# A causal tap filter and a gated two-layer product on one core: tap products dealt out between GEMM pairs, and loads, masks and transposes of the ramp rearranged

## The chip, the core and the metric

The kernel runs on one core of one Trainium2 chip. A core has a matrix engine (TensorE, PE in the profile; its weight loads are shown apart as PEld), a vector engine (VectorE, DVE), an engine for activation functions (ScalarE, ACT), a general engine that also issues transfers (GpSimd, POOL) and an engine that only issues transfers (SyncE, SP). They run on their own and wait for one another through semaphores; each takes its instructions in the order of the program. Data lie in HBM outside the core, in SBUF (128 partitions) and in PSUM, where TensorE writes its products. The metric is the device time of one execution in microseconds (us): 698.22, the median of three runs, 698.02 to 698.79.

## What is computed

The input x is 8 sequences of 4,096 tokens of 192 features. Every feature is filtered causally along the sequence with 7 taps; there are 8 sets of taps, one for each group of 24 features, normalised by a softmax. The result, as 32,768 tokens, goes through a layer to 2,048 features, through h * sigmoid(beta * h) with a beta for each of them, and back to 192:

```python
w = np.exp(weight - weight.max(-1, keepdims=True))
w = w / (w.sum(-1, keepdims=True) + 1e-09)              # (8 heads, 7 taps)
x_pad = concatenate([zeros(B, 6, D), x], axis=1)
x_unf = x_pad[:, idx, :].reshape(B, S, 7, 8, 24)        # idx: token + tap
t = einsum('hk,bskhg->bshg', w, x_unf).reshape(B * S, 192)
h = t @ w_in                                            # 192 -> 2048
out = (h / (1 + exp(-beta * h))) @ w_out                # 2048 -> 192
```

## The kernel before

**Tiles and steps.** The tokens are cut into two streams of 16,384 (s = 0, 1), which are worked on together: the 192 features are taken as 64 x 3, and the 64 rows of stream 0 and of stream 1 fill the 128 partitions. The list `steps` cuts each stream into steps of 128, 128 and 256 tokens (steps 0 to 2), then 256 (3 to 8) and then 512 (a tile). In each step the first GEMM gives 16 chunks of 128 hidden features, ScalarE applies Silu with beta as its scale (beta * h * sigmoid(beta * h), hence w_out is divided by beta), and the second GEMM of a step runs inside the next step, spread between that step's first-GEMM pieces by a plan (`mm2_plan`). Its product is copied to SBUF on VectorE (L368) and stored through SP.

**The filter has two forms.** For tile 0, that is steps 0 to 2, which are four blocks of 128 tokens (block 0 for step 0, block 1 for step 1, blocks 2 and 3 for step 2), TensorE does it: `transpose_0` (L202) transposes a block of x in fp32 by three matmuls with an identity, `take_0` (L209) copies it to SBUF as `xr[b]`, `halo_0` (L216) copies its last six tokens to the front of the next block, `conv_0` (L220) multiplies by seven diagonal matrices of the taps, two matmuls for each tap, and `evac_0` (L228) brings the sum to SBUF in bf16 (`xcp`). From tile 1 on VectorE does it: x is loaded in fp32 (`load_x`, L74), cast to bf16 (`cast_x`, L81), transposed by DMA (`transpose_x`, L91, issued on SP), and seven operations per step (L291, L293) multiply and add; the first of these steps is step 3. They are dealt out by `vector_work`, which runs them ahead by a budget in ns.

**Pairs.** In steps 0 to 2 `mm1_pair(i, u)` (L303) works on chunks u and u + 8 at once: six matmuls, three for each half of the partitions, then two activations (L314). The PSUM pool `psum_h` has two buffers, each for one pair. w_in comes in two halves: partitions 0 to 63 get the columns 0 to 1,023 and partitions 64 to 127 the columns 1,024 to 2,047 (`load_w_in`, L109, cast on the way). The other halves, which only steps from 3 on need, are copied within SBUF later (`copy_w_in`, L112).

**The ramp.** Taps, block 0 of x and beta are loaded first. POOL issues the first piece of w_in, builds two masks (`sel`, `ident`: clear, then select), issues the other three pieces, w_out, tile 1 in four loads and the w_in copies, and at last casts the second half of tile 1. SP loads blocks 1 to 3 of x. TensorE runs warm-up matmuls on zeros, the tap product, block 0's transposes, beta's transpose, three warm-ups, block 0's taps, five warm-ups, and then step 0. There, blocks 1 to 3 are transposed after pairs 0, 2 and 6, and the taps of blocks 1 and 2, 14 matmuls each, stand after pairs 1 and 4; those of block 3 stand after the first pair of step 1. `scale_w_out(c)` (L266) divides a chunk of w_out by beta on VectorE: eight chunks in step 0 from pair 4 on, four before and four after block 3's taps in step 1. The second GEMM of step 0 follows in step 1, its first phase after pairs 1 and 2, its second after pairs 5 to 7. The casts and DMA transposes of tile 1's first half stand after pair 4 of step 1, those of the second half after step 1.

Everything is issued through `pin`, so on each engine the order is that of the program's text. On POOL each of the later transfers waits until the transfer eight places before it on that queue has landed.

## Time and profile before

The profiled execution took 697.36 us; the span from its first instruction to its last is 695.6.

| engine | busy us | share of the span | instructions |
|---|---|---|---|
| TensorE matmuls | 686.9 | 99% | 11,559 |
| TensorE weight loads | 538.6 | 77% | 11,559 |
| ScalarE | 587.2 | 84% | 600 |
| VectorE | 541.8 | 78% | 901 |
| GpSimd | 13.7 | 2% | 26 |

A matmul's busy time overlaps that of its neighbours, so its sum says that TensorE is rarely without work, not that it runs at its peak. The granted TensorE clock is 1.000 over the span. The transfers of the ramp, issue and time to landing:

| transfer | queue | number, KB each | first issue | landed after, us |
|---|---|---|---|---|
| x, block 0, two halves | ACT, SP | 2, 96 | 0.73, 1.20 | 2.0 |
| beta | SP | 1, 8 | 1.61 | 3.2 |
| x, blocks 1 to 3 | SP | 3, 192 | 2.07 | 5.3 to 6.0 |
| w_in | POOL | 4, 192 | 1.26, 3.14 | 5.6 to 7.1 |
| w_out | POOL | 4, 384 | 5.02 | 7.7 to 9.1 |
| x, tile 1 | POOL | 4, 192 | 8.03 | 7.6 (median) |
| w_in copies | POOL | 4, 192 | 13.03 | 6.0 to 7.4 |

Over the 3 to 20 us from the span's start the 16 transfer engines are busy nearly all the time; between 5 and 7 us the queue of SP moved 320 packets (768 bytes each) per us, and the queue of POOL, casting w_in in packets of 1 KB, 62 to 132 per us from 6 to 9 us and 214 in the next.

### The profile page before, as it was taken

Reading aid. Unit: us, or ns where it says so; the run is one execution under the profiler, and the core shown is the slowest. Engines: PE = TensorE matmul, PEld = TensorE weight load, DVE = VectorE, ACT = ScalarE, POOL = GpSimd, SP = SyncE. Lnnn points to the kernel's source line nnn. Section 1 sums busy time; section 2 is a strip of 40 time slices with the busy share of each in tenths; the row PEclk is TensorE's granted clock in tenths of the full one; section 3 lists DMA queues with packets and bytes.
Section 4 is the critical chain, followed back from the end, with each engine's and each line's share of the span. In section 5 each row is a group of like instructions: output and inputs, shape, how many; then the busy total and the mean of one; then the engine's idle time right before and its main releaser. Section 6 shows DMA issues by size and latency. Waiting matters only on the chain.

```text
span 695.6 us, 25420 instructions
## 1 busy us (share of the span) xinstructions
PE 686.9 (99%) x11559; PEld 538.6 (77%) x11559; DVE 541.8 (78%) x901; ACT 587.2 (84%) x600; POOL 13.7 (2%) x26
## 2 busy tenths in 40 slices
PE   8999999999999999999999999999999999999998
PEld 6699996777777777777777777777777777777777
DVE  4799999999988788778798778797788797785002
ACT  5899999888888888888888888888888888888881
POOL 7000000000000000000000000000000000000000
PEclk9999999999999999999999999999999999999999
DMA  9654433443423334233334233334323342211112
GB/s 228 142 132 115 116 102 100 106 125 104 131 70 104 99 104 115 75 89 98 98 105 115 72 90 100 98 104 116 78 79 104 98 105 70 60 36 47 36 37 69
DMA packets 121196, 67.33 MB, mean 97 GB/s; under 512 B 55024, under 2 KB 120384, under 8 KB 121088
## 3 DMA queue, kind: packets, MB, share of 16 engines
q1 hardware_dynamic: 119152, 61.67, 32.8%
q0 software_dynamic: 1792, 3.93, 2.4%
q8 instruction: 90, 1.47, 0.9%
q14 instruction: 18, 0.15, 0.1%
q10 hardware_dynamic: 144, 0.10, 0.1%
HBM read 28.32 MB, written 25.17 MB: 77 GB/s over the span
## 4 chain that ended last, share of the span: by engine, by line
PE 92%; DVE 5%; DMA 1%; issue 1%; SPq 0%; POOL 0%; DVEq 0%; POOLq 0%
PE po L360 45%; PE ph L323 45%; DVE acc L293 3%; PE po L383 2%; DMA w_in_s<-in_moe_w_in_dram 1%; DVE w_out_s L267 1%; DVE xb L84 1%; PE po L224 0%; DVE acc L291 0%; DMA xt<-xb 0%; SPq L95 0%; DVE o_sb L368 0%; PE ph L310 0%; DVE xcp L235 0%; PE po L206 0%
## 5 line engine op out<-in xcount | busy, mean ns | idle before, releaser
L326 ACT ACTIVATE g<-ph,beta 128x1024 bf16<-128x1024 f32 (+1 forms) x544 | 560.8, 1039 | 85.0 <-PE ph L323 81.2
L360 PEld LDWEIGHTS <-g 64*128 64x128 bf16 x7936 | 361.1, 94 | 94.6 <-issue 1.3
L360 PE MATMUL po<-w_out_s,g 64*128 64x192 bf16 x7936 | 427.1, 243 | 0.7 <-DVE o_sb L368 0.5
L323 PE MATMUL ph<-xc,w_in_s 64*128 64x512 bf16 (+1 forms) x3264 | 419.0, 357 | 0.7 <-DVE xc L293 0.7
L293 DVE SCALAR_TENSOR_TENSOR acc<-xt,tapn,acc 128x512 f32<-128x512 bf16 (+1 forms) x450 | 315.4, 764 | 0.9
L323 PEld LDWEIGHTS <-w_in_s 64*128 64x128 bf16 x3264 | 167.7, 94 | 47.5 <-PE po L360 0.9
L368 DVE COPY o_sb<-po 128x384 f32<-128x384 f32 x124 | 69.1, 557 | 129.0 <-PE po L360 127.1
L293 DVE SCALAR_TENSOR_TENSOR xc<-xt,tapn,acc 128x512 bf16<-128x512 bf16 (+1 forms) x90 | 64.2, 765 | 0.2
L84 DVE CAST xb<-xf 128x768 bf16<-128x768 f32 (+1 forms) x62 | 49.0, 831 | 0.0
L291 DVE TENSOR_SCALAR acc<-xt,tapn 128x512 f32<-128x512 bf16 (+1 forms) x90 | 40.5, 501 | 3.0 <-DMA xt<-xb 1.9
L314 ACT ACTIVATE g<-ph,beta 128x256 bf16<-128x256 f32 (+1 forms) x48 | 22.0, 562 | 5.6 <-PE ph L310 5.2
L310 PE MATMUL ph<-xcp,w_in_s 64*128 64x256 bf16 (+1 forms) x144 | 14.5, 306 | 2.1 <-ACT g L314 1.5
L310 PEld LDWEIGHTS <-w_in_s 64*128 64x128 bf16 x144 | 6.9, 94 | 5.9 <-issue 3.4
L383 PE MATMUL po<-w_out_s,g 128*128 128x192 bf16 x128 | 10.7, 246 | 0.0
L383 PEld LDWEIGHTS <-g 128*128 128x128 bf16 x128 | 10.5, 98 | 0.2 <-issue 0.2
L386 DVE COPY o_sb<-po 128x192 f32<-128x192 f32 x8 | 2.9, 358 | 7.6 <-PE po L383 7.6
L235 DVE TENSOR_SCALAR xcp<-po,rsum 128x384 bf16<-128x384 f32 x7 | 4.0, 611 | 4.5 <-PE po L224 4.5
L224 PE MATMUL po<-xr,diag 64*128 64x384 f32 x49 | 7.1, 379 | 0.3 <-DVE xr L214 0.2
L224 PEld LDWEIGHTS po<-xr,diag 64*128 64x128 f32 x49 | 5.7, 204 | 1.1 <-DVE xr L214 1.1
L282 DVE COPY xt<-xt 128x18 bf16<-128x18 bf16 x28 | 4.7, 166 | 0.0
L267 DVE TENSOR_SCALAR w_out_s<-w_out_f,rbeta 128x192 bf16<-128x192 f32 x16 | 4.5, 353 | 0.0
L178 PE MATMUL ph<-zeros 128*128 128x256 bf16 (+1 forms) x16 | 3.1, 363 | 1.1 <-DVE xr L167 1.1
(44 smaller groups left out, 36.9 us busy)
## 6 DMA issues: line engine op xcount, KB each, us to landing
out_dram<-o_sb SPq DMA_DIRECT2D x124, 192.0 KB, 2.7
xf<-in_x_dram SPq DMA_DIRECT2D x60, 384.0 KB, 4.3
xt<-xb SPq DMA_TRANSPOSE x124, 2.4
w_out_f<-in_moe_w_out_dram POOLq DMA_DIRECT2D x4, 384.0 KB, 8.4
w_in_s<-in_moe_w_in_dram POOLq DMA_DIRECT2D x4, 192.0 KB, 6.6
xf<-in_x_dram POOLq DMA_DIRECT2D x4, 192.0 KB, 7.7
w_in_s<-w_in_s POOLq DMA_DIRECT2D x4, 192.0 KB, 7.0
out_dram<-o_sb SPq DMA_DIRECT2D x8, 96.0 KB, 1.6
```

The source lines that it names most:

```text
L84: pin((eng or nc.vector).tensor_copy(xbf_of[j][:, b0:b1, :, s, :].rearrange("p b k q -> p k b q"), xf_of[j][:, b0:b1, s, :].rearrange("p b ...
L224: pin(nc.tensor.matmul(cv[s][:, 0:NK * 128], diag[half_of(s), k, :, :].rearrange("p s q -> p (s q)"), xr[b][half_of(s), :, k:k + 128], sta ...
L267: pin(nc.vector.tensor_scalar_mul(w_out_s[:, c, :], w_out_f[:, c, :], rbeta[:, c:c + 1]))
L291: pin(nc.vector.tensor_scalar_mul(a, src, w))
L293: pin(nc.vector.scalar_tensor_tensor(out=xc_of[i][:, k0:k1, 0:n] if k == K - 1 else a, in0=src, scalar=w, in1=a, op0=ALU.mult, op1=ALU.add))
L310: pin(nc.tensor.matmul(ph[:, h, 0:NS * n], w_in_s[half_of(h), kk, ts(fcs[h], 128)], xc_of[i][half_of(h), :, kk, :], start=(kk == 0), stop= ...
L314: pin(nc.scalar.activation(g_of[i][:, fcs[h], :, 0:n], ph[:, h, 0:NS * n].rearrange("p (s t) -> p s t", s=NS), AF.Silu, scale=beta[:, fcs[ ...
L323: pin(nc.tensor.matmul(ph[:, s, 0:n], w_in_s[half_of(s), kk, ts(fc, 128)], xc_of[i][half_of(s), kk, 0:n], start=(kk == 0), stop=(kk == NK ...
L326: pin(nc.scalar.activation(g_of[i][:, fc, :, 0:n], ph[:, :, 0:n], AF.Silu, scale=beta[:, fc:fc + 1]))
L360: pin(nc.tensor.matmul(po[:, q, 0:D], g_of[i][r, fc, s, ts(b, 128)], w_out_s[r, fc, :], start=(phase == 0 and fc == 0), stop=(phase == 1 a ...
L368: pin(nc.vector.tensor_copy(o_sb, po[:, :, 0:D]))
L383: pin(nc.tensor.matmul(po[:, 0, 0:D], g_of[i][:, fc, s, ts(b, 128)], w_out_s[:, fc, :], start=(fc == 0), stop=(fc == NF - 1)))
```

## The change

- **Loads.** Block 1 of x is loaded on SP after beta; blocks 2 and 3 go to POOL's queue. w_in comes in six pieces instead of four (256, 384 and 384 columns of each half), and blocks 2 and 3 stand behind the second pair of pieces. The load of beta stays where it was.
- **Masks.** `sel` and `ident` are cleared on VectorE; POOL only selects, and issues its first w_in piece after that.
- **Beta.** Its transpose on TensorE and the copy move behind block 0's convolution, and into the unused bank of the warm-ups.
- **Warm-ups.** Four in place of three before block 0's taps, and none in place of five after them.
- **Blocks.** Block 1's transposes stand before step 0, those of blocks 2 and 3 after pairs 0 and 1. Two banks, `pa` and `pb`, serve in turn for the transposes and the taps.
- **Taps.** Block 1's seven taps are dealt out as 1, 3 and 3 after pairs 1, 2 and 3; block 2's as 2, 3 and 2 after pairs 4, 5 and 6; block 3's as 4 and 3 after pairs 3 and 4 of step 1.
- **w_out.** Scaled after pairs 5 and 7 of step 0 and pairs 0 and 1 of step 1, four chunks each.
- **Tile 1.** Its first half is transposed in fp32 on TensorE after pair 6 of step 1 and copied to bf16 by VectorE; the two DMA transposes and two VectorE casts for it go. The second half is cast on VectorE instead of POOL, after pair 7 of step 1, and transposed by DMA; then the loads of tiles 2 and 3.

```diff
+    load_x0(1, nc.sync)
...
-    load_w_in(0, 0, 512)
-    for b in range(1, NB):
-        load_x0(b, nc.sync)
...
-    pin(nc.gpsimd.memset(sel, 0.0))
+    pin(nc.vector.memset(sel, 0.0))
...
-    pin(nc.gpsimd.memset(ident, 0.0))
+    pin(nc.vector.memset(ident, 0.0))
...
-    for f in range(0, HF, 512):
+    for f0, f1 in ((0, 256), (256, 640), (640, HF)):
         for s in range(NS):
-            if f or s:
-                load_w_in(s, HF * s + f, HF * s + f + 512)
+            load_w_in(s, HF * s + f0, HF * s + f1)
+        if f0 == 256:
+            for b in range(2, NB):
+                load_x0(b, nc.gpsimd)
...
-    for s in range(NS):
-        cast_x(1, s, 2, 4, nc.gpsimd)
...
-    def transpose_0(bank, b):
+    def transpose_0(bank, b, src=x0):
...
-    def conv_0(cv, b):
-        for k in range(K):
+    def conv_0(cv, b, k0=0, k1=K):
+        for k in range(k0, k1):
...
-    po01 = po_tile()
-    t0_ = transpose_0(po01[:, 0, :], 0)
-    take_0(t0_, 0, act=True)
-    po_b = po_tile()
-    beta_ps = po_b[:, 1, 0:NF]
-    pin(nc.tensor.transpose(beta_ps, beta16, ident[0:NF, 0:NF]))
-    beta = consts.tile([128, NF], FP32, name="beta")
-    pin(nc.vector.tensor_copy(beta, beta_ps))
+    pa = po_tile()
+    t = transpose_0(pa[:, 0, :], 0)
+    take_0(t, 0, act=True)
+    warm(4, 128)
     for k in range(2, K):
         make_diag(k)
     rsum = consts.tile([128, 1], FP32, name="rsum")
     pin(nc.vector.reciprocal(rsum, tsum))
-    warm(3, 128)
+    halo_0(t, 0)
...
+    pb = po_tile()
+    b0 = [cv0[:, 0, :], pb[:, 0, :]]
     conv_0(b0, 0)
     evac_0(b0, 0, 0, nc.scalar)
     evac_0(b0, 0, 1, nc.vector)
-    warm(5, 128)
+    beta_ps = idle[:, 1, 0:NF]
+    pin(nc.tensor.transpose(beta_ps, beta16, ident[0:NF, 0:NF]))
+    beta = consts.tile([128, NF], FP32, name="beta")
+    pin(nc.vector.tensor_copy(beta, beta_ps))
+    t = transpose_0(pa[:, 0, :], 1)
+    take_0(t, 1)
+    halo_0(t, 1)
...
+            cv1, cv2, cv3 = banks(pb), banks(pa), banks(pb)
             for u in range(NF // 2):
                 mm1_pair(0, u)
                 if u == 0:
-                    t = transpose_0(po01[:, 1, :], 1)
-                    take_0(t, 1)
-                    halo_0(t, 1)
+                    t = transpose_0(pb[:, 0, :], 2)
+                    take_0(t, 2)
+                    halo_0(t, 2)
                 elif u == 1:
-                    cv = banks(po_tile())
-                    conv_0(cv, 1)
-                    for s in range(NS):
-                        evac_0(cv, 1, s, nc.vector)
+                    t = transpose_0(pa[:, 0, :], 3)
+                    take_0(t, 3)
+                    halo_0(t, 3)
+                    conv_0(cv1, 1, 0, 1)
+                elif u == 2:
+                    conv_0(cv1, 1, 1, 4)
+                elif u == 3:
+                    conv_0(cv1, 1, 4, K)
+                    for s in range(NS):
+                        evac_0(cv1, 1, s, nc.vector)
+                elif u == 4:
+                    conv_0(cv2, 2, 0, 2)
+                elif u == 5:
+                    conv_0(cv2, 2, 2, 5)
+                    for c in range(4):
+                        scale_w_out(c)
+                elif u == 6:
+                    conv_0(cv2, 2, 5, K)
+                    for s in range(NS):
+                        evac_0(cv2, 2, s, nc.vector)
+                elif u == 7:
+                    for c in range(4, 8):
+                        scale_w_out(c)
...
-                if i == 1 and u == 0:
-                    for c in range(8, 12):
+                if i == 1 and u < 2:
+                    for c in range(8 + 4 * u, 12 + 4 * u):
                         scale_w_out(c)
-                    cv = banks(po_tile())
-                    conv_0(cv, 3)
-                    for c in range(12, NF):
-                        scale_w_out(c)
+                elif i == 1 and u == 3:
+                    conv_0(cv3, 3, 0, 4)
+                elif i == 1 and u == 4:
+                    conv_0(cv3, 3, 4, K)
                     for s in range(NS):
-                        evac_0(cv, 3, s, nc.vector)
+                        evac_0(cv3, 3, s, nc.vector)
+                elif i == 1 and u == 6:
+                    pt = po_tile()
+                    new_xt(1)
+                    for b in range(2):
+                        t = transpose_0(pt[:, b, :], b, xf_of[1])
+                        pin(nc.vector.tensor_copy(
+                            xt_of[1][:, :, LEAD + 128 * b:LEAD + 128 * b + 128], t))
+                elif i == 1 and u == 7:
+                    for s in range(NS):
+                        cast_x(1, s, 2, NB)
+                    for b in range(2, NB):
+                        transpose_x(1, b)
+                    for s in range(NS):
+                        load_x(2, s)
+                    for s in range(NS):
+                        load_x(3, s)
                 for t in plan[2 * u] + plan[2 * u + 1]:
                     mm2(i - 1, *t)
-                if i == 1 and u == 4:
-                    for s in range(NS):
-                        cast_x(1, s, 0, 2)
-                    for b in range(2):
-                        transpose_x(1, b)
...
-            if i == 1:
-                for s in range(NS):
-                    load_x(2, s)
-                for b in range(2, NB):
-                    transpose_x(1, b)
-                for s in range(NS):
-                    load_x(3, s)
             continue
```

## The prediction

> **What bounds the kernel now.** I read the busy time by stage first, then the chain of waits in order of time, then the timeline of the first 50 us. In the table each row has a stretch in us, its length, and the busy time of PE, PEld, DVE, ACT and POOL:
>
> ```profile
> 3.00:9.00 6.00, 5.22 (x29) 3.89 (x29) 3.28 (x15) 2.91 (x6) 5.79 (x9) 1.00 1.06 180
> ...
> 16.00:20.00 4.00, 3.60 (x43) 2.68 (x41) 3.84 (x13) 3.02 (x8) 1.63 (x4) 1.00 1.04 268
> 20.00:26.00 6.00, 5.40 (x110) 4.83 (x107) 4.04 (x12) 4.81 (x13) 0.47 (x1) 1.00 0.19 47
> 26.00:36.00 10.00, 8.64 (x118) 5.35 (x114) 7.63 (x10) 9.72 (x18) 0.00 (x0) 1.00 0.86 197
> 36.00:47.00 11.00, 10.99 (x230) 10.85 (x231) 10.79 (x15) 10.72 (x17) 0.00 (x0) 1.00 0.39 94
> ...
> 100.00:680.00 580.00, 580.00 (x9713) 441.69 (x9710) 455.81 (x752) 496.47 (x449) 0.00 (x0) 1.00 0.33 90
> ```
>
> From 36 us to the end TensorE is full and the change doesn't touch that code: all that can be won or lost is when step 3 starts (36 us), and one later stall. Between 26 and 36 ScalarE is full (9.72 of 10). The chain names what lies before (start, length, what):
>
> ```profile
> 3.14 6.49 DMA w_in_s<-in_moe_w_in_dram
> ...
> 17.30 0.92 DVE w_out_s L267 x4
> 18.22 0.47 DVE xr L214
> 18.68 0.08 DVE xt L218
> 18.77 3.42 DVE w_out_s L267 x12
> 22.19 1.05 DVE xcp L235 x2
> ...
> 26.35 2.36 DMA xt<-xb
> ```
>
> So the first GEMM pair waits for w_in until 9.64, VectorE leads from 17 to 24 us, and the transpose of tile 1 leads VectorE's taps (seven, to 35.87), for which step 3 waits. The timeline adds:
>
> ```profile
> 5.11 0.50 PE L178 MATMUL ph<-zeros 128*128 128x128 bf16 x3
> ...
> 14.61 1.51 PE L224 MATMUL po<-xr,diag 64*128 64x384 f32 x14
> ...
> 18.41 0.69 POOL L84 CAST xb<-xf 128x384 bf16<-128x384 f32 x1 [1.15 <-DMA xf<-in_x_dram]
> ...
> 26.98 9.35 ACT L314 ACTIVATE g<-ph,beta 128x512 bf16<-128x512 f32 x16 [0.28 <-PE ph L310]
> ...
> 47.59 0.51 PE L360 MATMUL po<-w_out_s,g 64*128 64x192 bf16 x8 [0.53 <-DVE o_sb L368]
> ```
>
> **Unit prices**, as distances between starts in that timeline: a pair of step 0 or 1 is 0.33 us before another pair, 0.43 before an fp32 operation; three transposes 0.55; 14 tap matmuls 1.34, that is 0.085 each and 0.16 per block; a second-GEMM matmul 0.042; eviction L235 0.57; cast of a block to xr 0.56; w_out scaling 0.2275.
>
> **1. Up to block 0's convolution.** The masks are cleared on VectorE (its memsets are 0.06 to 0.17 us, free at 1 us) so POOL's two selects end near 2.0, not 3.19. TensorE's transposes started at 3.39, but x0's block 0 landed only at 1.20 + 2.0 = 3.2: gain 0.1. Beta's transpose held TensorE until 4.89 and VectorE (beta copy) until 5.21; it moves behind the convolution. That now starts when ScalarE's xr is there (4.83 less 0.1, plus 0.1 to see it), 4.85 instead of 5.54, with four warm matmuls hidden before it. VectorE makes seven diagonals from 4.0 at 0.284 (1.42/5), faster than the convolution's 0.32 a tap. It lasts 2.61 as before (5.54 to 8.15): end 7.45, **0.7 earlier**.
>
> Here a rule is to be weighed. Row: block 0's taps are 0.32 apart, block 1's 0.19, both at granted clock 1.00. The Trainium skill ("TensorE: Matmul & The Clock Gate", Part 1) says that TensorE runs at half rate until one window of about 3.4 us has been busy. Before, TensorE idled from 4.30 to 4.89; after, no gap over 0.3 is left from 1.05 on, so by the rule the rate doubles by 1.05 + 2 x 3.4 = 7.9 at the latest, 6.2 on average, and the convolution would end at 6.6 (bounded by the diagonals). By the row 7.45. I take the row; step 3 tells why the other changes little.
>
> **2. First pair.** Evictions end at 8.1 (were 8.84); beta's transpose and block 1's (0.18 + 0.65 of weight loads, still slow) end at 8.3. The five removed warm matmuls (0.71) were hidden. w_in's first two loads now hold 256 of 1,024 columns instead of 512. Before, all four loads took from the first packets (2.7, 1.45 after the issue) to 11.5 (4.40 + 7.1), less 2.4 for three x0 blocks beside them (768 packets at 320 per us, the 5 to 7 us rate): 6.4. Now the first issue comes at 2.05, packets from 3.5; both first pieces land at 3.5 + 6.4/4 + 0.8 (x0 block 1) = 5.9, or, if a packet costs the same at any length, 7.5. Either way before 8.3: the 0.63 wait goes. Pair 0 at **8.3, was 9.68**.
>
> **3. Step 0, where the gain stops.** TensorE: seven pairs 3.01, two block transposes 1.10, taps in blocks of 2, 6, 6, 4, 6, 4 matmuls 3.34: 7.45, so block 2's taps would end at 15.75 (were 16.12). ScalarE needs 0.76 a pair against about 1.0 here and hides. But x0's blocks 2 and 3 leave SP for POOL's queue, behind four w_in loads, and pair 1 stands behind block 2's transposes. Block 2 is wanted at 8.73. It lands at 3.5 + 5/8 of 6.4 + 1.6 (two x0 blocks) = 9.1 by bytes; by packets (768 short ones in front, 6.4) at 11.5. Bounds 9.1 and 11.5. I take 9.7: the x0 packets of 768 bytes went at 320 per us, so shorter packets are cheaper, but not in proportion. Block 3 comes 0.8 later and is wanted 0.98 later: hidden. Wait 0.97, and 0.1 for VectorE to leave the bank before the first tap: **taps end at 16.8, 0.7 later than before**.
>
> A second rule of the Trainium skill speaks against this move: "SBUF — State Buffer", "A bandwidth-pool intuition that's wrong", says GpSimd can't write descriptors while a two-port VectorE operation holds their shared port, and advises the other queues. Row: POOL's w_in issues took 0.63 and w_out's 0.81 both beside the diagonals (4.09 to 6.73) and after them. By the row nothing; by the rule four issues each behind one 0.28 diagonal, 1.1 on x0 and all that follows. I take the row.
>
> **4. Step 1.** VectorE evicts block 2 (16.9 to 18.05), then scales chunks 4 to 15. Before, twelve took 3.51, since two of them (0.54 and 0.756 against a median of 0.309) met POOL's casts; those casts are gone: 11 x 0.2275 + 0.31 = 2.8, so the first phase of the second GEMM ends at 20.95 (was 22.3). w_out's last load landed by 16.6 before; 1 us later still hides. What TensorE has behind it has grown: block 3's taps, formerly at 18.74 under the scaling, now stand behind it, with two fp32 transposes of tile 1. Pair 0.43 + 8 taps 0.84 + pair 0.43 + 6 taps 0.67 + pair and 12 matmuls 0.74 + pair 0.43 + transposes 1.10 + 10 matmuls 0.45 + 0.75 = 5.84, where before 3.74 were left. Step 2 starts at **26.8, was 26.06**.
>
> Moved w_in copies stay last on POOL's queue; landing near 24.5 against a first use in step 3: hidden. Tile 1's casts and last DMA transposes move to 27 us on SP, ahead of loads and the store: two transposes lasted 3.5, wanted by step 4's taps near 36.5. Its second-GEMM bank is now the one that the first store's copy frees: VectorE's two xt copies, two casts and that copy end near 27.5, TensorE asks at 26.8 + 0.83: hidden by 0.1.
>
> **5. Step 2 and on.** ScalarE starts 0.92 after TensorE and takes 9.35: 37.05, where before step 3's first activation was at 36.62: **0.43 late**. The DMA transpose (1.88 of VectorE waiting) no longer matters: the taps begin at 27.8, end near 35, step 3's first pair runs before ScalarE is free. VectorE is then 0.9 earlier and TensorE 0.43 later than before, so the 0.53 stall at 47.59 (a copy queued behind taps) goes, with 0.13 more in 58 to 70. Sum: +0.43 - 0.53 - 0.13 = **-0.2**. The profiled execution took 697.36 (span 695.6 and 1.76 around it), the median 698.22, 0.86 more; the difference carries over: 698.0.
>
> **Rivals.**
> - *Block 2 in time.* w_in's bytes count, the clock doubles as the rule has it, and x0 lands by 8.1: pair 0 at 7.7, taps end at 15.2, 1.6 before mine: -1.8, **696.4**. For it: no idle gap left. Against: even the byte price gives 9.1; with that alone -0.8.
> - *The queue behind w_in* (the other side). Packets count, not bytes: x0 at 11.5, everything after 1.8 later: +1.6, **699.8**. It decides from a landing of 11.3 on. For it: w_in's packets ran at only 62 to 132 per us before 9 us. Against: x0's short packets were fast.
> - *The clock stays low.* Without the five warm matmuls a window counts as idle, and one more window of 3.4 runs at half rate: 1.7 later, **699.7**. Against: TensorE has work throughout.
> - *Dealing out does nothing*, as ScalarE was never starved: unchanged, 698.2; against it are its waits before 13.29, 16.50 and 20.63 (1.25, 0.67, 1.10), which TensorE's block of taps caused.
>
> **How the numbers follow.** Less than 0.2% (1.4 us) can't be told from no change; the three times shown spread over 0.8. Forecast 0.55 (its own range 697.0 to 699.3), block 2 in time 0.23, queue 0.14, clock 0.07, nothing 0.01. Range 696.4 to 699.9. Faster by over 0.2% 0.24 (the second case and an edge of the first), slower 0.20, between 0.56.
>
> **What would show it.** Conv of block 0 ends near 7.45; pair 0 near 8.3; an idle TensorE of about 1 us before block 2's transposes, released by a DMA; scaling at 0.23 apart; block 3's taps after the first phase of the second GEMM; step 2 near 26.8; VectorE without a wait for xt; no stall at stage 4. I am wrong if x0 is on time or over 1.6 late, or if the later stall stays.

## The result, and the profile after

The changed kernel took 695.69 us in the median of four executions (695.60 to 695.77), beside 698.42 of the kernel before (four executions, 698.02 to 698.79): a ratio of 0.9961 (0.9944 to 0.9978 with 95% confidence; intervals stand in brackets from here on). The forecast was 698.0, its range began at 696.4: the kernel became faster by more than was held likely. Its profiled execution took 695.62 (span 693.8), 1.74 less than that of before. The later runs were made in four groups, each on one chip beside fresh executions of before (medians 697.86 to 698.07); in them 12 more executions of the changed kernel gave a median of 695.63 and 0.9972 [0.9961, 0.9982]. Three of these twelve took 697.50 to 697.93, the rest 695.47 to 695.94; other kernels have such long executions too, so medians are compared.

First the busy time by stage in the kernel after, with the same columns as in the prediction's first fence (stretch, length, then PE, PEld, DVE, ACT, POOL):

```profile
20.00:26.00 6.00, 5.22 (x80) 4.23 (x78) 2.87 (x6) 3.66 (x9) 0.00 (x0) 1.00 0.18 45
26.00:36.00 10.00, 9.22 (x128) 5.81 (x123) 9.75 (x14) 9.72 (x19) 0.00 (x0) 1.00 0.64 183
```

These two rows tell where to look. Between 20 and 26 VectorE has 2.87 of work, before it had 4.04, and ScalarE 3.66 in place of 4.81: here TensorE leads, and the others wait for it. Between 26 and 36 VectorE has no gap any more (9.75, before 7.63): its wait for the DMA transpose is gone.

To follow the gain through the kernel I put the start of every activation of before beside that of after. ScalarE stands between the two GEMMs, so its starts show what is late at each point:

```
activation           before   after    after - before
0   (step 0, pair 0)  10.22    9.15    -1.07
12  (step 0, pair 6)  17.23   15.18    -2.05
20  (step 1, pair 2)  21.61   18.32    -3.29
28  (step 1, pair 6)  25.12   22.86    -2.26
32  (step 2)          26.98   26.80    -0.18
50  (step 3)          37.89   37.40    -0.49
66  (step 4)          49.12   47.95    -1.17
82  (step 5)          59.94   58.49    -1.45
590 (last tile)      679.72  678.25    -1.47
```

Up to 3.3 us are won in the first 18 us, and all but 0.2 of it is given back before step 2. What counts in the end is won after that, at three places: the start of step 3, and the stalls of steps 4 and 5. Another 0.3 lies behind the last activation.

**Where it is won.** TensorE's timeline of after (start, length, instruction; in brackets the wait and what ended it):

```profile
8.61 0.50 PE L308 MATMUL ph<-xcp,w_in_s 64*128 64x256 bf16 x6
9.51 0.61 PE L200 MATMUL po<-ident,x 128*128 128x128 f32 x3 [0.39 <-DMA x<-in_x_dram]
10.05 0.50 PE L308 MATMUL ph<-xcp,w_in_s 64*128 64x256 bf16 x6
10.48 0.61 PE L200 MATMUL po<-ident,x 128*128 128x128 f32 x3
...
12.17 0.51 PE L308 MATMUL ph<-xcp,w_in_s 64*128 64x256 bf16 x6
12.43 0.80 PE L217 MATMUL po<-xr,diag 64*128 64x384 f32 x6
```

The first pair starts at 8.61 in place of 9.68, without a wait for w_in. TensorE then waits for block 2 of x, which POOL's queue brings behind w_in: issued at 4.43, landed 5.03 later, at 9.46. Compare the distances: a pair before three transposes takes 0.43 (10.05 to 10.48), a pair before taps only 0.26 (12.17 to 12.43). In before every block of taps behind a pair waited for VectorE's cast of x to `xr`, so that no row of it shows a pair before taps without a wait. The weight loads of block 2's taps in before:

```profile
14.61 1.19 PEld L224 LDWEIGHTS po<-xr,diag 64*128 64x128 f32 x14 [0.21 <-DVE xr L214]
```

VectorE's timeline of after continues behind TensorE's:

```profile
15.53 1.14 DVE L228 TENSOR_SCALAR xcp<-po,rsum 128x384 bf16<-128x384 f32 x2 [0.17 <-PE po L217]
16.59 2.83 DVE L265 TENSOR_SCALAR w_out_s<-w_out_f,rbeta 128x192 bf16<-128x192 f32 x12
21.70 1.14 DVE L228 TENSOR_SCALAR xcp<-po,rsum 128x384 bf16<-128x384 f32 x2 [2.28 <-PE po L217]
```

Twelve chunks of w_out are scaled in 2.83 (before 3.51 in the same view) and are through at 19.4, 2.8 earlier than before. Then VectorE is idle for 2.28: it waits for block 3's taps, which TensorE reaches only now.

**Where it is given back.** All engines of after around the transposes of tile 1:

```profile
23.25 0.28 PE L200 MATMUL po<-ident,xf 128*128 128x128 f32 x1
23.56 0.56 DVE L471 CAST xt<-po 128x384 bf16<-128x384 f32 x1 [0.72 <-PE po L200]
24.17 0.62 PE L200 MATMUL po<-ident,xf 128*128 128x128 f32 x3 [0.65 <-DVE xt L471]
...
25.68 0.84 ACT L312 ACTIVATE g<-ph,beta 128x256 bf16<-128x256 f32 x2 [1.98 <-PE ph L308]
...
26.78 0.75 DVE L289 TENSOR_SCALAR acc<-xt,tapn 128x768 f32<-128x768 bf16 x1
26.80 1.26 ACT L312 ACTIVATE g<-ph,beta 128x512 bf16<-128x512 f32 x2 [0.28 <-PE ph L308]
```

The second transpose writes the other bank of the same PSUM tile, yet it starts only when VectorE has copied the first (24.17; TensorE waits 0.65, its weight loads 0.84). ScalarE waits 1.98 for the pair behind it. From the end of the second GEMM's first phase to step 2 TensorE takes 6.33 (pair at 19.56, step 2's first at 25.89).

**What makes the end earlier.** The waits of TensorE that the profile lists between 33 and 75 us, first in before, then in after, are all of these (a smaller one at step 5 of before, 0.3, is seen only in the starts):

```profile
36.01 0.50 PE L323 MATMUL ph<-xc,w_in_s 64*128 64x256 bf16 x6 [0.71 <-DVE xc L293]
47.59 0.51 PE L360 MATMUL po<-w_out_s,g 64*128 64x192 bf16 x8 [0.53 <-DVE o_sb L368]
```

```profile
36.20 0.50 PE L321 MATMUL ph<-xc,w_in_s 64*128 64x256 bf16 x6 [0.32 <-ACT g L312]
```

Before, step 3 waited for VectorE's taps (xc), whose start had waited 1.88 for the DMA transpose. After, the taps start at 26.78 in place of 28.79, step 3 waits for ScalarE instead, and VectorE is early enough that the stall at 47.59 is not there.

### The profile page after: what moved, and what is told of

Read it like the earlier page. It is cut to its first block, busy times and chain, and to the rows that moved or that the text cites. A ratio compares the mean times of both kernels' runs of the same rounds, so it can differ in the third digit from the quotient of the medians.

```text
span 693.8 us, 25426 instructions
## 1 busy us (share of the span) xinstructions
PE 686.7 (99%) x11561; PEld 537.6 (77%) x11561; DVE 542.3 (78%) x905; ACT 587.4 (85%) x600; POOL 14.5 (2%) x26
## 4 chain that ended last, share of the span: by engine, by line
PE 96%; ACT 2%; DMA 1%; POOL 0%; issue 0%; DVE 0%; POOLq 0%; ACTq 0%
PE po L358 47%; PE ph L321 46%; ACT g L312 2%; PE po L381 2%; DMA x<-in_x_dram 1%; PE ph L308 1%; PE po L217 0%; POOL w_in_s L110 0%; PE po L200 0%; DVE xt L471 0%; POOL sel L143 0%; DVE o_sb L384 0%; POOL ident L145 0%; POOLq L143 0%; POOLq L145 0%
## 5 line engine op out<-in xcount | busy, mean ns | idle before, releaser
L110 POOL DMA_DIRECT2D w_in_s<-in_moe_w_in_dram x6 | 3.9, 648 | 0.0
```

## The experiments

In what follows "before" and "after" are the two kernels. Diffs are against after where the label begins with a or best, against before where it begins with b.

**1. Is the difference of 0.86 between before's profile and its median a constant?** No edit: before once more.

> The kernel before, once more, to see what its own executions differ by. Theory: its timed executions hold about 1 us more than the one profiled (698.0 to 698.8 against 697.36), from something in the first 60 us that varies from run to run; then this profile lies anywhere from 697.3 to 698.8, and where it is longer the place shows (step 2, 3, 4 or 5 begins later against 26.98, 36.62, 48.46, 59.28). Rival: a profiled execution of this kernel is always 0.9 shorter; then it is 697.3 to 697.5 again while the timed ones are at 698.4.

Median 697.82 of 11 (697.25 to 698.88), ratio 0.9997 [0.9988, 1.0005]. Its profiled execution took 698.06. The chain of waits of that execution has

```profile
1.61 4.45 DMA beta<-in_moe_beta_dram
6.07 0.04 issue
6.11 0.28 PE po L246
```

The same 8 KB took 4.45 to land, where the first profile had 3.2. Block 0's taps stood behind beta's transpose and began at 6.76 instead of 5.54; the first activation started 0.52 later, step 2's 0.75 later, and it ended 0.70 later. So the profile of 697.36, from which the sum was made, lies low among the executions of a kernel that spread over 1.6 us, and its 0.86 below the median is that scatter, no constant part of an execution. In after nothing stands behind beta until block 0's taps are through; what that is worth in the medians no run shows, since the only test of this move alone, experiment 10, came out slower for another reason.

**2. The changed kernel once more**, with the same question.

> The changed kernel once more, timed beside the others. Theory A: its own executions are closer together than those of the kernel before (whose first pair waits for w_in or beta, which land at different times), most at 695.5 to 696.0; one in four to ten may lie 2 us higher, where TensorE keeps its low rate past 9 us as the DMA-transpose variant's profile did to 14.4. Theory B: no such mode here, all within 0.4, and the median advantage over before stays at 2.7 as first measured rather than about 2.2.

Median 695.63, profile 695.47: nine of twelve within 0.5 us, three 2 us above. In its trace TensorE gets its full rate later than in the first profile of after: the three transposes at 7.65 still take 0.91 and the pair at 8.49 0.82, and only block 2's transposes, at 9.26, take 0.61. The end is not later for it, since TensorE has to wait for block 2 of x until about then in any case.

**3. Are the dealt-out taps worth anything?** Blocks 1 and 2 get their 14 tap matmuls in one go again:

```diff
-                    conv_0(cv1, 1, 0, 1)
-                elif u == 2:
-                    conv_0(cv1, 1, 1, 4)
-                elif u == 3:
-                    conv_0(cv1, 1, 4, K)
+                    conv_0(cv1, 1)
                     for s in range(NS):
...
-                    conv_0(cv2, 2, 0, 2)
+                    conv_0(cv2, 2)
+                    for s in range(NS):
+                        evac_0(cv2, 2, s, nc.vector)
```

> The changed kernel with the taps of blocks 1 and 2 undivided again (7 after pair 1, 7 after pair 4, each evicted at once); block 3's stay dealt out. Theory A, dealing out brings the gain: ScalarE waits again by 1.2 and 0.7 us in step 0, all comes later by 0.5 to 1.5, 696.2 to 697.2. Theory B, VectorE's scaling of w_out leads step 1 and what is won in step 0 is given back before step 2: block 2 is evicted and scaled sooner, step 2 starts no later than 26.8, 695.0 to 695.8.

Median 697.49 of 12 (696.51 to 699.11), 0.9992 [0.9983, 1.0002]; 1.9 above after. In the profile (696.52) step 2 starts 0.87 later than in after, although block 2's transposes started 0.20 earlier (9.31), and this stays to the end. ScalarE's timeline in this kernel, then in after:

```profile
12.75 2.30 ACT L312 ACTIVATE g<-ph,beta 128x256 bf16<-128x256 f32 x6 [1.51 <-PE ph L308]
15.77 4.72 ACT L312 ACTIVATE g<-ph,beta 128x256 bf16<-128x256 f32 x12 [0.72 <-PE ph L308]
```

```profile
11.85 7.31 ACT L312 ACTIVATE g<-ph,beta 128x256 bf16<-128x256 f32 x18 [0.42 <-PE ph L308]
```

With the taps in one piece ScalarE is starved twice (1.51 and 0.72) and TensorE then waits for it; dealt out, ScalarE runs 18 activations in a row. The dealing out is worth 0.9 in the profiles. The medians show 1.9: four of the twelve lie at 696.5 to 696.7, like the profile, the rest spread up to 699.11, three of these with a granted clock of 0.997 or 0.998; what makes them longer wasn't found.

**4. Do the transposes on TensorE pay?** Tile 1's first half goes back to VectorE casts and DMA transposes after pair 4; the block after pair 6 goes:

```diff
-                elif i == 1 and u == 6:
-                    pt = po_tile()
...
+                if i == 1 and u == 4:
+                    for s in range(NS):
+                        cast_x(1, s, 0, 2)
+                    for b in range(2):
+                        transpose_x(1, b)
```

> The changed kernel with tile 1's first half cast on VectorE and transposed by DMA after pair 4 of step 1, as before. Theory A, the TensorE transposes pay: step 2 starts 2 us earlier (about 24.0 on TensorE), but step 3 waits for VectorE's taps again until about 35.9, and the stall at step 4 of 0.5 to 0.7 returns: 695.7 to 696.5. Theory B, they only cost TensorE and VectorE 2 us: step 3 starts near 34.4, 693.9 to 694.3.

Median 696.37 of 12 (nine between 695.93 and 696.85, three between 698.32 and 698.59), 0.9975 [0.9964, 0.9986]: 0.7 above after. The profile is that of a long execution (698.43): TensorE stayed at half rate to 14.4 (last section), and from pair 6 of step 0 to the end of step 1 everything is 2.30 later than in after. VectorE's and then TensorE's timeline:

```profile
29.80 0.75 DVE L289 TENSOR_SCALAR acc<-xt,tapn 128x768 f32<-128x768 bf16 x1 [2.49 <-DMA xt<-xb]
```

```profile
37.02 0.50 PE L321 MATMUL ph<-xc,w_in_s 64*128 64x256 bf16 x6 [1.65 <-DVE xc L291]
```

TensorE's tail before step 2 is short without the transposes (4.25 in place of 6.33), and it gains nothing: VectorE waits 2.49 for the DMA, its taps lead step 3, as in before. At step 2 this execution was 0.23 later than after's, at step 5 2.45. Not all of that belongs to the DMA transposes. With the 2.30 of the slow start taken off, an estimate from these two profiles, the taps start at 27.5 where after's start at 26.78, and the end is 0.5 later, in line with the 0.7 of the medians. No trace shows a shorter execution of this kernel.

**5. Is the tail the place of the loss?** Two edits together: block 3's taps move forward, after pairs 0 and 1 of step 1, under VectorE's scaling; and both transposes of tile 1 are issued ahead of both copies.

```diff
                 if i == 1 and u < 2:
+                    conv_0(cv3, 3, 4 * u, 4 + 3 * u)
...
-                elif i == 1 and u == 3:
-                    conv_0(cv3, 3, 0, 4)
-                elif i == 1 and u == 4:
-                    conv_0(cv3, 3, 4, K)
-                    for s in range(NS):
-                        evac_0(cv3, 3, s, nc.vector)
+                    if u:
+                        for s in range(NS):
+                            evac_0(cv3, 3, s, nc.vector)
...
+                    ts_ = [transpose_0(pt[:, b, :], b, xf_of[1]) for b in range(2)]
                     for b in range(2):
-                        t = transpose_0(pt[:, b, :], b, xf_of[1])
                         pin(nc.vector.tensor_copy(
-                            xt_of[1][:, :, LEAD + 128 * b:LEAD + 128 * b + 128], t))
+                            xt_of[1][:, :, LEAD + 128 * b:LEAD + 128 * b + 128], ts_[b]))
```

> The changed kernel with block 3's taps after pairs 0 and 1 of step 1, where TensorE waits for the scaling of w_out, and with the two fp32 transposes of tile 1 ahead of both copies, so that the second doesn't wait for the first's copy. Theory A, TensorE leads from the end of the scaling (19.5) to step 2 and 1.25 + 0.84 us of it are gone: step 2's first activation at 24.8 instead of 26.8, step 3's at 34.0, 693.6 to 694.0. Theory B, VectorE's evictions and copies take the lead at once: no more than 0.8 is gained, 694.9 to 695.7.

Median 694.23 of 6 (five between 693.89 and 694.39, one 696.02), 0.9944 [0.9931, 0.9957]: 1.4 below after, faster than both. Lines of TensorE's and of ScalarE's timeline:

```profile
16.07 0.98 PE L217 MATMUL po<-xr,diag 64*128 64x384 f32 x8
...
22.12 0.95 PE L200 MATMUL po<-ident,xf 128*128 128x128 f32 x6
```

```profile
23.96 0.84 ACT L312 ACTIVATE g<-ph,beta 128x256 bf16<-128x256 f32 x2 [0.90 <-PE ph L308]
25.08 9.36 ACT L312 ACTIVATE g<-ph,beta 128x512 bf16<-128x512 f32 x16 [0.28 <-PE ph L308]
```

The six transposes run in one stretch, ScalarE waits 0.90 in place of 1.98, and step 2 starts at 25.08, 1.72 before that of after. All of the 1.72 is still there at the end. 0.24 of it was there before these edits act, since block 2 of x landed earlier (its transposes start at 9.25); about 1.5 is theirs.

**6. The wait for the first copy alone.** Only the second of those two edits.

> The changed kernel with both fp32 transposes of tile 1 ahead of both copies. Theory A: the second no longer waits 0.65 to 0.84 for the first's copy, step 2's first activation at 26.0 to 26.2 instead of 26.8, and the end as much earlier, 694.8 to 695.1. Theory B: another wait (the last activation of step 1, the store's copy) takes the place, 695.4 to 695.8.

Median 695.06 of 6, 0.9956 [0.9940, 0.9972]. In the profile (694.78) step 2 starts at 25.98, 0.82 before that of after, and the end is 0.84 earlier. Counted from pair 6 of step 0, which leaves out when x landed, this one wait is worth 0.9 and block 3's place 0.6; the medians put them at 0.6 and 0.8.

**7. x0's place in the queues.** Blocks 2 and 3 of x go back to SP.

```diff
-    load_x0(1, nc.sync)
+    for b in range(1, NB):
+        load_x0(b, nc.sync)
...
-        if f0 == 256:
-            for b in range(2, NB):
-                load_x0(b, nc.gpsimd)
```

> The changed kernel with x's blocks 2 and 3 on SP's queue again. Theory A, they are late only because they stand behind w_in on POOL's queue: block 2 lands by 8.2, the wait of 0.67 before its transposes goes, and because step 0 is bound by TensorE from there until ScalarE is full, up to 0.7 is gained, 694.9 to 695.3. Theory B, the transfers' sum decides: w_in's pieces land later instead and a pair waits for w_in, no change or up to 1 slower, 695.6 to 696.8.

Median 695.91 of 5, 0.9962 [0.9950, 0.9975]: no gain. TensorE's timeline:

```profile
8.49 0.82 PE L306 MATMUL ph<-xcp,w_in_s 64*128 64x256 bf16 x6
9.24 0.80 PE L198 MATMUL po<-ident,x 128*128 128x128 f32 x3
9.98 0.50 PE L306 MATMUL ph<-xcp,w_in_s 64*128 64x256 bf16 x6
```

The wait for x is gone, but the pair and the transposes take 0.82 and 0.80 where after has 0.50 and 0.61: TensorE got its full rate later, at about 9.8, and block 2's transposes start only 0.27 earlier than in after (9.24 against 9.51). So the two profiles differ in the rate too and don't give the price of the queue alone. The second profile of after (experiment 2) had the same late rate, and there block 2's transposes start at 9.26: between these two the place in the queue is worth nothing. Experiment 12 gives its price where the full rate comes earlier, 0.34. The forecast had priced it at 0.97.

**8. POOL's casts.** The second half of tile 1 is cast on POOL again, at the end of its queue.

```diff
+    for s in range(NS):
+        cast_x(1, s, 2, 4, nc.gpsimd)
...
-                    for s in range(NS):
-                        cast_x(1, s, 2, NB)
```

> The changed kernel with the second half of tile 1 cast on POOL again, as before, at the end of POOL's queue. Theory A, those casts stretch the scalings of w_out beside them: one or two of twelve take 0.5 to 0.76 instead of 0.31, the twelve last 3.3 to 3.5 instead of 2.83, and all comes 0.3 to 0.7 later (two VectorE casts of 0.45 behind them are saved but hidden): 696.0 to 696.4. Theory B, the scalings are done before POOL casts: no difference, 695.5 to 695.8.

Median 695.95 of 9, 0.9975 [0.9963, 0.9987]. POOL's, then VectorE's timeline:

```profile
19.92 0.69 POOL L84 CAST xb<-xf 128x384 bf16<-128x384 f32 x1 [2.26 <-DMA xf<-in_x_dram]
20.82 0.70 POOL L84 CAST xb<-xf 128x384 bf16<-128x384 f32 x1 [0.20 <-DMA xf<-in_x_dram]
```

```profile
16.72 2.83 DVE L267 TENSOR_SCALAR w_out_s<-w_out_f,rbeta 128x192 bf16<-128x192 f32 x12
```

Here the scaling is over (19.55) before the casts begin, and takes the same 2.83 as in after. With the rest of the change in place, the move of the casts to VectorE brings nothing.

**9. The same move in before**, where the casts did lie beside the scaling:

```diff
-    for s in range(NS):
-        cast_x(1, s, 2, 4, nc.gpsimd)
...
+                for s in range(NS):
+                    cast_x(1, s, 2, 4)
```

> The kernel before with the second half of tile 1 cast on VectorE behind step 1 in place of POOL. Theory A, VectorE's scaling of w_out, stretched by POOL's casts from 2.83 to 3.51, led the kernel before: step 2 and VectorE's taps begin 0.6 to 0.7 earlier, median 0.4 to 0.7 below before's. Theory B: TensorE or the DMA transpose lead there, no change (within 0.2 of before).

Median 697.49 of 11, 0.9988 [0.9980, 0.9997], 0.6 below before. VectorE's timeline of this kernel, then of the second profile of before, which began nearly alike (first activation at 10.96 and 10.74):

```profile
19.49 2.83 DVE L265 TENSOR_SCALAR w_out_s<-w_out_f,rbeta 128x192 bf16<-128x192 f32 x12
...
28.75 0.75 DVE L289 TENSOR_SCALAR acc<-xt,tapn 128x768 f32<-128x768 bf16 x1 [0.47 <-DVE xt L280]
```

```profile
19.21 3.72 DVE L267 TENSOR_SCALAR w_out_s<-w_out_f,rbeta 128x192 bf16<-128x192 f32 x12
...
29.51 0.75 DVE L291 TENSOR_SCALAR acc<-xt,tapn 128x768 f32<-128x768 bf16 x1 [1.86 <-DMA xt<-xb]
```

The scaling takes 0.9 less; tile 1's taps start 0.76 earlier, and the last tile's activations are 0.75 earlier. So in before the end follows the start of VectorE's taps for tile 1.

**10. Beta's move alone**, done in before:

```diff
-    beta_ps = po_b[:, 1, 0:NF]
-    pin(nc.tensor.transpose(beta_ps, beta16, ident[0:NF, 0:NF]))
-    beta = consts.tile([128, NF], FP32, name="beta")
-    pin(nc.vector.tensor_copy(beta, beta_ps))
...
     evac_0(b0, 0, 1, nc.vector)
+    beta_ps = idle[:, 1, 0:NF]
+    pin(nc.tensor.transpose(beta_ps, beta16, ident[0:NF, 0:NF]))
...
     warm(5, 128)
```

> The kernel before with beta's transpose and copy alone moved behind block 0's taps. Theory A: beta lands at 4.8 in one profile of the kernel before and at 6.06 in the other, and TensorE held for it; moved, the taps end at 7.5 in all executions and the first pair waits for w_in alone (9.6 and later): the lowest time stays (697.2 to 697.4), the median falls by 0.3 to 0.7 and the upper half comes closer. Theory B: w_in varies as much as beta; median and spread stay as before's.

Median 699.61 of 11 (699.20 to 700.40), 1.0023 [1.0014, 1.0032]: slower, against both theories. TensorE's timeline:

```profile
8.32 0.69 PE L178 MATMUL ph<-zeros 128*128 128x128 bf16 x5 [0.61 <-DVE beta L258]
8.94 1.08 PE L310 MATMUL ph<-xcp,w_in_s 64*128 64x256 bf16 x6
9.95 0.91 PE L206 MATMUL po<-ident,x 128*128 128x128 f32 x3
...
11.51 2.61 PE L224 MATMUL po<-xr,diag 64*128 64x384 f32 x14
```

Block 0's taps are through 0.65 earlier, as they should. But everything behind them is at half rate until about 15.2: 14 taps take 2.61, where before took 1.53. The warm matmuls here wait for beta's copy (0.61), but whether this gap is what holds the rate down stays open: in experiment 11's variant of this kernel the gap is the same and the rate was full at 8.3.

**11. Does the number of warm matmuls set the rate?** `warm(4, 128)` before block 0's taps becomes 3 (a_warm3) and 6 (a_warm6), and 6 with experiment 5's edits (best_warm6), and `warm(3, 128)` becomes 6 with experiment 10's (b_beta_warm6).

> The changed kernel with 3 warm matmuls before block 0's taps instead of 4: 0.11 us less of dense work. Theory A, whether TensorE's rate doubles near 7.6 hangs on how long the stretch of dense matmuls up to the end of block 0's taps is (about 3.4 us with four warm-ups, and three of twelve executions miss it; 3.3 with three, as in the kernel before with beta moved, where all missed it): most or all executions at 697.3 to 698.0, and TensorE's transposes at 0.9 until 14 us. Theory B, the slow executions come by chance[...]: no more than four in ten, median 695.5 to 696.0.

> The changed kernel with 6 warm matmuls there: 0.21 us more, still ended when ScalarE's xr is there (4.85). Theory A: none or one of the executions is slow, all at 695.4 to 696.0. Theory B: as the changed kernel, two to four in ten at 697.5.

> Block 3's taps after pairs 0 and 1 of step 1 and both transposes ahead of both copies, with 6 warm matmuls: 693.9 to 694.4 in all executions, ratio to before about 0.994 (theory A of both); or the same median with one in six 2 us higher (theory B).

> The kernel before with beta's transpose moved and 6 warm matmuls instead of 3 before block 0's taps. Theory A, moving beta cost 1.75 only since it took the dense stretch away from TensorE: with six the rate doubles again near 7.6, the first pair waits for w_in alone, median 697.2 to 697.6, below before's 697.9 and with fewer executions above 698.5. Theory B, the hold for beta's copy after the taps does it: slow still, 699.2 to 700.4.

Three: 695.92 of 6, 0.9969 [0.9957, 0.9980]. Six: 695.91 of 6, 0.9968 [0.9955, 0.9980]. Neither differs from after by more than 0.3, and in the profiles the full rate came no earlier with six (a tap at 7.20 still takes 0.52) than with three (0.34 at 6.88): no run here shows that their number sets the rate. On top of experiment 5, six gave 695.57 of 5, 0.9959 [0.9947, 0.9972], beside 694.23 without: two of the five (694.20, 694.59) are as fast, three 1.4 to 2 us longer, and the intervals overlap, so that six is not shown to be worse. On top of experiment 10 it gave 698.98 of 11, 1.0013 [1.0003, 1.0022], 0.6 better, with intervals that overlap as well. The profile of best_warm6 is one of its long executions; TensorE's timeline:

```profile
5.52 0.33 PE L217 MATMUL ph<-xr,diag 64*128 64x384 f32 x1
...
7.22 0.50 PE L308 MATMUL ph<-xcp,w_in_s 64*128 64x256 bf16 x6
9.59 0.61 PE L200 MATMUL po<-ident,x 128*128 128x128 f32 x3 [1.86 <-DMA x<-in_x_dram]
...
12.15 1.31 PE L217 MATMUL po<-xr,diag 64*128 64x384 f32 x6
...
15.85 0.78 PE L217 MATMUL po<-xr,diag 64*128 64x384 f32 x6
```

In this execution the full rate came early (taps of 0.33 at 5.5), so the first pair was at 7.22. TensorE then waited 1.86 for block 2 of x, which came no sooner, at 11.3 the rate fell to half (six taps in 1.31), and at 14.75 it came back.

**12. The best two together**: experiments 5 and 7.

> Block 3's taps under the scaling, both transposes ahead of both copies, and x's blocks 2 and 3 on SP's queue. Theory A, the slow executions come from TensorE's wait for x[...]: without that wait none lies 2 us above the others, all 693.8 to 694.5. Theory B: one in four to six still lies at 696.

Median 694.00 of 6 (693.10 to 695.23), 0.9933 [0.9920, 0.9946]: the fastest, but its median is not told apart from that of experiment 5 alone (694.23). The two profiles differ in x's place alone and both have the full rate from the first pair on. TensorE's timeline here, then in experiment 5:

```profile
8.91 0.61 PE L198 MATMUL po<-ident,x 128*128 128x128 f32 x3
```

```profile
9.25 0.61 PE L200 MATMUL po<-ident,x 128*128 128x128 f32 x3 [0.42 <-DMA x<-in_x_dram]
```

Block 2 is in time, its transposes start 0.34 earlier, step 2 0.35 (24.73), and the last tile 0.34. By this pair of profiles, that is what POOL's queue costs.

## Why the prediction was wrong, step by step

The forecast for the profiled execution was 697.36 - 0.2 = 697.2, the measured 695.62, so of its miss of 2.3 us 1.54 lies in the sum and 0.8 in the step from the profile to the median. The two signs by which it wanted to be known as wrong, x0 on time or over 1.6 late, and a later stall that stays, did not come: it was wrong in the size of its terms and in a wait that it left out.

1. **Block 0's convolution**: forecast end 7.45, measured 7.77. The mechanism held. 0.24 went to block 0 of x, which landed later than in before's profile: TensorE waited for it until 3.71, where in a_x0_sp it began at 3.40, and its last taps at 6.98. The row for the rate (0.32 a tap) held in this execution, and the rule's 6.6 did not. It was not a safe choice: in best_warm6 the rate rose early, and block 0's taps were through at 6.4.
2. **First pair**: forecast 8.3, measured 8.61, with w_in in time. Held, with the 0.3 of step 1.
3. **Step 0**: block 2's landing, forecast at 9.7, measured 9.46: held, and with it the value chosen between bytes (9.1) and packets (11.5). POOL's two issues of x took 0.73 and 0.74 beside VectorE's diagonals, no longer than the loads of tile 1 later (0.72 each), so the 1.1 of the second rule was not there; whether the diagonals are operations of the kind that it means, no run shows. Then comes the step that failed first: taps through at 16.8 by the forecast, 15.3 by the same way of counting (pair 7 starts at 15.32, VectorE evicts at 15.53). **"Seven pairs 3.01" took 0.43, the price of a pair before three transposes, for the pairs before taps as well.** Five of them took 0.26: 5 x 0.17 = 0.85. The six blocks of taps took 3.01 (0.29 + 0.61 + 0.62 + 0.44 + 0.61 + 0.44), not 3.34, another 0.33, and the 0.1 for the bank was not there. That is 1.28 of the 1.48; the rest is x's landing. The unit price was read from one neighbour and used beside another, and before had no clean row for the other, since its taps behind a pair waited each time for VectorE's cast (0.21 to 0.50 by the weight loads).
4. **Scaling and the tail**: scaling forecast at 2.8, measured 2.83: held, for the wrong reason. It was credited to the casts' move, but in after the scaling is so early that the casts would miss it anyway (experiment 8); in before it does pay 0.6 (experiment 9). The first phase of the second GEMM was through 1.4 earlier than forecast (pair at 19.56 against 20.95), carried on from step 3. **The tail, forecast at 5.84, took 6.33.** Two pairs before taps were 0.36 cheaper, for the reason of step 3, and eight and six taps 0.08; but the transposes took 1.78 instead of 1.10, as the second waits for the first's copy; the pair ahead of them took 0.62 instead of 0.43 (they write the PSUM tile of block 3's taps, which VectorE left at 22.84); and the rest took 0.06 more, where a pair with 12 matmuls had been given 0.74, the price of one with 10. The sum named every instruction in the tail and missed this wait between two engines; experiment 6 puts it at 0.8 to 0.9. Step 2's activations started at 26.80, forecast 27.7 (26.8 + 0.92).
5. **Step 3 and on**: forecast "0.43 late" against before, measured 0.49 early: step 2 came 0.9 earlier than forecast, and this carries on. ScalarE leads there, for 9.35, as forecast, and the DMA transpose's wait is gone. The stall at 47.59 went, as forecast; this and a smaller one at step 5 were worth 0.68 and 0.28, 0.96 together, where 0.53 + 0.13 were counted. 0.3 more came from the last store's landing, which no step spoke of.
6. **"The difference carries over: 698.0."** It did not. The 0.86 was scatter of before (experiment 1: its second profile was 0.70 longer, 0.52 of it before the first activation, from beta's landing and the taps that stood behind it). After's profiled execution is within 0.1 of its median.

Of the rivals, *block 2 in time* (696.4) came nearest with its number, but not with its mechanism: block 2 was late, as in the forecast, and where it is in time (experiment 12) this is worth 0.34. That the number lay near was luck. *The clock stays low* (699.7) did not occur in either profile of after; a loss of its size may stand behind the three of twelve executions that took 2 us longer, but that the missing warm matmuls cause it is not shown. *The queue behind w_in* fell with the landing at 9.46. *Dealing out does nothing* fell: it is worth 0.9 in the profiles and 1.9 in the medians.

So of 3.3 us won before 18 us only 0.2 reaches step 2, since block 3's taps (1.3, formerly hidden under the scaling) and tile 1's transposes were put where TensorE alone sets the pace. What remains at the end, 1.5 in the profile, is that tile 1's taps start 2.0 earlier on VectorE, whose chain led step 3 in before, until ScalarE leads instead. Two things bring this about: the work on VectorE ahead of the taps is done earlier, and they no longer wait for a DMA transpose. The transposes on TensorE alone are worth 0.5 to 0.7 (experiment 4), the dealing out 0.9 to 1.9 (experiment 3); the shares need not add up. Experiments 5 and 6 confirm the reading of the tail: what it is shortened by arrives whole at the end. Open is the rest of the medians' 2.3 to 2.7, of which this pair of profiles, with a short execution of before, shows 1.74: beta's landing gave 0.7 in one profile, and more was not traced.

## What to carry to other kernels

A unit price belongs to a pair of neighbours: read the distance to the next instruction of the kind that will really follow, free of waits that the change removes, or the error is multiplied by the count. Move work to where an engine waits for another (here TensorE under VectorE's scaling), not behind the point at which it becomes the one that leads, and issue all producers of a two-buffer exchange before the first consumer. And before a sum is made on a single profile, look at what in it depends on a landing: a second execution of the same kernel was 0.7 us longer through one load of 8 KB.

## What the hardware showed that was not expected

**TensorE's rate changes at times that the kernel alone doesn't set, and it can stay low for long.** The two profiles of after, the same kernel, had the full rate by 7.9 and only near 9.2. The profile of a_dma_xt is one of the long executions; TensorE's timeline:

```profile
9.79 0.91 PE L200 MATMUL po<-ident,x 128*128 128x128 f32 x3 [0.47 <-DMA x<-in_x_dram]
...
13.23 1.31 PE L217 MATMUL po<-xr,diag 64*128 64x384 f32 x6
...
14.74 0.78 PE L217 MATMUL po<-xr,diag 64*128 64x384 f32 x6
```

TensorE had work from 1.05 on, with no wait over 0.5 from 4.9, and still ran at half rate until about 14.4. Its step 1 is 2.3 later than after's, about the distance of the long executions from the others. That all of these have to do with the rate is not shown, since the timed executions leave no trace but their granted clock. This much speaks for it: ten executions of after and of experiments 4, 5 and 8 are 1.5 us or more above the fastest of their kernel; five of them have a granted clock of 0.997 or 0.998, as have the two profiles in which the rate fell again, and none of the other 29 is under 0.999. In best_warm6 the rate rose near 4.55, fell near 11.3 and rose near 14.75; in b_beta_warm6 it fell near 10.8 and rose near 14.2. The last two distances are 3.4 to 3.45, and 6.75 is twice that: they fit the window of about 3.4 us over which, by the Trainium skill, TensorE's rate is judged ("TensorE: Matmul & The Clock Gate", Part 1), and which by that page runs freely and doesn't begin with the kernel; two traces are too few to show more. But its rule that one sustained window brings the full rate, from which the prediction had "7.9 at the latest", fits after's profile and not a_dma_xt's or b_beta's, and the rate fell after windows that were by no means idle: best_warm6's had 1.86 of waiting in 3.4, b_beta_warm6's 0.66 and 0.85.

**The granted clock doesn't show the low start.** It is 1.000 over a_dma_xt's span and over b_beta's, at half rate to 14.4 and 15.2, and 0.997 and 0.998 in the two profiles in which the rate fell again (best_warm6, b_beta_warm6). Whether TensorE is at half rate at the start is read from the distances of equal matmuls (0.32 or 0.17 per tap), not from that number.

**A faster start need not win.** In its profile best_warm6 had its first pair 1.4 us before after's and still took 695.98, where experiment 5's profile took 693.89 without the two extra warm matmuls: it only came sooner to a load that hadn't landed, and after that wait the rate fell. That the wait made it fall is likely and not shown.
